# Float64 weights split by other VectorE and ScalarE operations without GpSimd, in a static issue order planned anew

## The chip, the cores and the metric

The kernel runs on one core of a Trainium2 chip. The metric is the device time of one execution in microseconds (us), as the median of several runs. TensorE is PE (PEld is its weight load), VectorE is DVE, ScalarE is ACT, GpSimd is POOL, and SyncE (SP) issues the transfers.

## The reference, cut to what matters

```
q, k = rotate(q), rotate(k)                    # rope; batch 2, 8 heads, 576 tokens, head size 64
attn = softmax(q @ k.T / 8) @ v                # (sum + 1e-9 below), float32
x = attn, heads side by side                   # 1152 x 512
h = x @ w_in                                   # 512 x 2048, float64 weights
g = h if h >= 1; 0 if h <= -1; else (h + 1)**2 / 4
x = (g @ w_out).astype(float32)                # 2048 x 512, float64 weights
p = domain_probs / (row sum + 1e-9)            # 1152 x 4
out = sum over 4 experts e of p[:, e] * (relu(x @ w1[e]) @ w2[e])   # inner width 1024, float32
```

## The kernel before

**Products.** Each operand of a product is cut into two float32r parts, high (h) and low (l), and each product is three matmuls: h·h, l·h, h·l. Activations stand as XH and XL, weights as pairs of tiles such as w00h and w00l.

**Units.** Attention works on 8 pairs of heads. For each: rope of k and q, their split, transposes, scores (tile `sc`), row maxima (`nm`), exponentials on ACT (`E`), transposed probabilities (`pt`, copied to `PT` and `PU`), the product with v (`av`), its scaling (`avx`) and its split to XH and XL. Probability sums take a round trip through DRAM (`rt`, `rdram`, `rbs`). The last product of attention is av71 (pair 7, second half). The feed-forward part has 12 chunks of the inner width: chunks 0 to 3 are the first layer pair (512 columns of `w_in` and 512 rows of `w_out` each), chunks 4 to 11 the four experts. Tokens stand in three column blocks of 384. A unit is one chunk and one block, once for the inward product (`pi`, four groups of twelve 128x384 matmuls) and once for the outward product (`po`). That makes 72 units. We write pi0_1 for chunk 0, block 1, and pi0_1_3 for its fourth group.

**After a pi group** of chunks 0 to 3 come two ACT operations (g?a), a DVE operation that reads PSUM (L438, g?b), an ACT cast (hid?h, L440) and a subtraction on POOL (hid?l, L441). A po group of chunks 1 to 3 is added to ACC on DVE (L478).

**Weights.** A float32 weight slice of 512 columns is split by one ACT copy and one DVE subtraction (L344). Float64 weights (32 slices, eight for each of chunks 0 to 3, four of `w_in` and four of `w_out`) arrive as pairs of 32-bit words in `wrawa` or `wrawb`, and `w_split` cuts each slice with the temporary tiles wt0 or wt1 (u and y each): L365 to L368 on DVE build a float32 y from the high words, ACT copies y to the h part (L381), L372 and L373 on DVE make the low words' value in u, POOL takes h from y (L377) and adds u to what remains (L385), which gives the l part. Chunk 0's slices are split during attention, the 24 others after it, in what we call the stage: from the end of av71 to the start of po2_0, the first outward unit of chunk 2.

**Order.** Every operation is registered with `op(engine, ns, priority, ...)`, and the class `Plan` runs a list scheduler over them before the program is emitted: its cost functions (`mm_ns`, `act_ns`, `dve_ns`, `pool_ns`), the constant LAT and the priorities in `CFG` fix in which order instructions stand on each engine and queue. Each engine then runs its list in that order. Tiles in rings (`Ring`) rotate. Phase 1 is what may only be issued once phase 0, attention, has been.

Of the kernel before, what the change touches and what calls it, by code (L numbers as in the profile page):

```python
# [10 lines left out]
F32 = mybir.dt.float32  # L11
# [7 lines left out]
P = 128  # L19
# [66 lines left out]
class Ring:  # L86
    """A rotating buffer: tiles take its slots in the order in which they are issued."""
# [24 lines left out]
class Op:  # L112
    __slots__ = ("eng", "ns", "fn", "prio", "bufs", "need", "outs", "ready", "lat", "seq", "phase", "start", "cols")


class Plan:
    """Static issue order: ops with their engine, length and data; a list scheduler over them."""

    LAT = 200.0
# [6 lines left out]
    def op(self, eng, ns, prio, fn, reads=(), writes=(), bufs=(), lat=0.0, phase=0, cols=None):  # L126
        o = Op()
        o.cols = ns * 2.37 if cols is None else cols
        o.eng, o.ns, o.fn, o.prio, o.bufs, o.lat, o.phase = eng, ns, fn, prio, bufs, lat, phase
# [12 lines left out]
        for d in deps:  # L142
            d.outs.append(o)
        o.need = len(deps)
        for b in bufs:
            b.left += 1
        self.ops.append(o)
        return o

    def order(self):  # L150
# [13 lines left out]
        heat, heat_to = CFG["fill"], CFG["fill_to"]  # L164

        def est(o):
            t = max(free[o.eng], o.ready)
# [12 lines left out]
            return t  # L180

        while len(out) < n:
# [72 lines left out]
def fused_kernel(ctx: ExitStack, tc, q, k, v, w_in, w_out, dprobs, w1, w2, tab, out):  # L255
# [67 lines left out]
    def w_split(c, kind, a, prio, phase, slot, tmp, after=()):  # L323
# [12 lines left out]
        def l():  # L336
            return part(1)

        if not is_wide(c):
            def t():  # L340
# [4 lines left out]
                l(), t(), h().bitcast(F32), op=ALU.subtract), [rk, hk], [lk], wb, phase=phase)  # L345
# [15 lines left out]
        def c1():  # L361
# [3 lines left out]
            nc.vector.tensor_scalar(uu, hi, 0x7FFFFFFF, None, op0=ALU.bitwise_and)  # L365
# [4 lines left out]
        def c2():  # L370
            u, y = uy()
            nc.vector.tensor_scalar(u.bitcast(U32), y.bitcast(U32), 0xFF800000, None, op0=ALU.bitwise_and)  # L372
            nc.vector.scalar_tensor_tensor(u, lohi()[0], 2.0 ** -52, u, op0=ALU.mult, op1=ALU.mult)  # L373

        def c3():
            y = uy()[1]
# [3 lines left out]
        op("DVE", 3 * dve_ns(512, True) + dve_ns(512) + 380, prio, c1, [rk], [uk, yk], phase=phase)  # L380
        op("ACT", act_ns(512, True), prio, lambda: nc.scalar.copy(h(), uy()[1]), [yk, *after], [hk], wb, phase=phase)  # L381
        op("DVE", dve_ns(512, True) + dve_ns(512) + 130, prio, c2, [rk, yk], [uk], phase=phase)
        op("POOL", pool_ns(512), prio, c3, [hk], [yk], phase=phase)
        e, ns = (nc.gpsimd, pool_ns(512)) if (CFG["ladd"][phase == 1] >> a & 1) else (nc.vector, dve_ns(512))
        op("POOL" if (CFG["ladd"][phase == 1] >> a & 1) else "DVE", ns, prio, lambda: e.tensor_tensor(l(), uy()[1], uy()[0], op=ALU.add),  # L385
           [yk, uk, hk], [lk], wb, phase=phase)
# [61 lines left out]
    def out_unit(c, b, d, ring, prio, phase):  # L448
# [82 lines left out]
        "PT0": Ring(kp, "PT0", 2, [P, 2, 4, 256], F32),  # L531
# [32 lines left out]
    def plan_pair(n):  # L564
# [23 lines left out]
        # loads  # L588
# [39 lines left out]
        def rope(x, eng, lo, hi, pr):  # L628
# [22 lines left out]
            op(engs[0], nss[0], pr, m1, rk + tk, sk, [raws[x], rot[x]])  # L651
            op(engs[1], nss[1], pr, m2, rk + tk, [(t2, lo)], [raws[x], t2])
            op(engs[2], nss[2], pr, m3, [(t2, lo)], sk, [rot[x], t2])

        def split_h(x, lo, hi, pr):
# [3 lines left out]
            if first:  # L659
# [14 lines left out]
            op("DVE", dve_ns(512, True) + dve_ns(64), pr, fn, rk, hk, [rot[x], hls[x]])  # L674

        def split_l(x, lo, hi, pr):
# [9 lines left out]
                op=ALU.subtract), rk + hk, lk, [rot[x], hls[x]])  # L686
# [102 lines left out]
        # scores, softmax, transposed probabilities  # L789
# [11 lines left out]
        def tile_step(s):  # L801
# [85 lines left out]
        def av(g):  # L887
# [13 lines left out]
            op("DVE", 270 + 75 * g, g0 + O["rd"], rd, [(sm, s) for s in range(lo, hi)], [r], [sm, r])  # L901
# [46 lines left out]
            op("DVE", dve_ns(256, True) + g * 102, te + O["xh"], xh, [ax], hk, [ax])  # L948
# [32 lines left out]
    # the tail columns of both batches form one column tile  # L981
# [25 lines left out]
    op("DVE", 790, 24, norm_probs, ["dpt"], ["probs"], phase=2)  # L1007
# [104 lines left out]
```

## Time and profile before

| | |
|---|---|
| median of 3 runs | 832.33 us (831.71 to 832.98) |
| the profiled execution, first to last instruction (span) | 831.0 us; no other time of that execution is given, and the median is 1.3 us above it |
| PE busy | 774.3 us (93%) |
| DVE, ACT, POOL busy | 476.5, 294.4, 257.5 us |
| bytes moved by transfers | 51 MB, 61 GB/s in the mean |

PE is busy in most of the span, but the share is a mean over stages: the span falls into attention (to 194.46 us), the stage that splits the rest of the float64 weights (to 340.78 us) and a rest of some 490 us.

### The profile page before, as it was taken

To read this page: it belongs to the slowest core of one execution; us is meant where nothing else is said; L and a number is where in the kernel's file an instruction comes from. 1 tells how busy PE (TensorE), PEld (TensorE's weight loads), DVE (VectorE), ACT (ScalarE), POOL (GpSimd) and SP (SyncE) were. 2 spreads that over 40 slices of the span, in tenths; PEclk is the share of its full clock that TensorE was granted. 3 is DMA by queue.
4 is the path that set the end of the run, shared out by engine and by line. 5 is a ranking of instruction groups with operands and counts; after the bars stand their busy time and mean duration, and the time that the engine had idled before them with its cause. 6 is when DMAs were issued, how large, how long until landed. Compare 5 with 4: busy or idle time off the path is not lost.

```text
span 831.0 us, 11155 instructions
## 1 busy us (share of the span) xinstructions
PE 774.3 (93%) x4310; PEld 691.4 (83%) x4310; DVE 476.5 (57%) x752; ACT 294.4 (35%) x663; POOL 257.5 (31%) x224
## 2 busy tenths in 40 slices
PE   5899999999876687799999999999999999999997
PEld 4677667789776687799999989998899899989996
DVE  6978798978999999734333333332433333332222
ACT  3677667664333332345531121220222121120110
POOL 4788773456656666522520000000000000000000
PEclk9999999999889999799999999999999999999999
DMA  5334333213232131211001111101111101000012
GB/s 162 96 97 125 97 75 108 82 67 108 95 102 101 52 102 50 102 52 51 26 26 50 51 52 51 44 8 50 51 51 52 38 14 51 1 1 1 1 38 77
DMA packets 38789, 51.08 MB, mean 61 GB/s; under 512 B 7624, under 2 KB 22288, under 8 KB 38736
## 3 DMA queue, kind: packets, MB, share of 16 engines
q1 hardware_dynamic: 38656, 50.04, 19.0%
q8 instruction: 34, 0.56, 0.3%
q0 software_dynamic: 80, 0.33, 0.2%
q14 instruction: 19, 0.16, 0.1%
HBM read 43.60 MB, written 2.40 MB: 55 GB/s over the span
## 4 chain that ended last, share of the span: by engine, by line
PE 73%; DVE 21%; issue 2%; ACT 1%; POOL 1%; DMA 1%; SPq 0%; DVEq 0%; POOLq 0%; ACTq 0%
PE pi L414 31%; PE po L466 30%; PE av L926 4%; PE sc L816 4%; PE pt L851 3%; DVE wt0u L366 2%; DVE wt1u L366 2%; DVE wt1u L365 2%; DVE wt0u L365 2%; DVE nm L833 1%; DVE wt0u L367 1%; DVE wt1u L367 1%; DVE XH L942 1%; DVE wt1y L368 1%; DVE wt0y L368 1%
## 5 line engine op out<-in xcount | busy, mean ns | idle before, releaser
L414 PE MATMUL pi<-XH,w 128*128 128x384 f32 x576 | 155.5, 345 | 18.8 <-DVE g2b L438 9.6
L414 PEld LDWEIGHTS pi<-XH,w 128*128 128x128 f32 x576 | 107.4, 191 | 21.3 <-DVE g2b L438 10.2
L414 PE MATMUL pi<-XH,w00h 128*128 128x384 f32 x288 | 98.0, 340 | 12.3 <-DVE g1b L438 9.4
L499 DVE SCALAR_TENSOR_TENSOR ACC<-po,ptile,ACC 128x512 f32<-128x512 f32 x63 | 47.3, 751 | 106.9 <-PE po L466 106.8
L414 PE MATMUL pi<-XL,w 128*128 128x384 f32 x288 | 99.0, 344 | 0.0
L414 PE MATMUL pi<-XH,w00l 128*128 128x384 f32 x288 | 97.1, 337 | 0.0
L414 PE MATMUL pi<-XL,w00h 128*128 128x384 f32 x288 | 97.0, 337 | 0.0
L414 PEld LDWEIGHTS pi<-XH,w00h 128*128 128x128 f32 x288 | 54.6, 190 | 14.6 <-DVE g1b L438 9.7
L833 DVE TENSOR_REDUCE nm<-sc 128x1 f32<-128x576 f32 x72 | 53.6, 748 | 14.7 <-PE sc L816 13.5
L466 PE MATMUL po<-w,hid0h 128*128 128x512 f32 x192 | 60.5, 396 | 0.0
L838 ACT ACTIVATE E<-sc,nm 128x576 f32<-128x576 f32 x72 | 53.6, 745 | 16.7 <-DVE nm L833 16.4
L466 PE MATMUL po<-w,hid2h 128*128 128x512 f32 x192 | 59.3, 390 | 0.0
L466 PE MATMUL po<-w,hid1h 128*128 128x512 f32 x192 | 59.3, 390 | 0.0
L414 PEld LDWEIGHTS pi<-XL,w 128*128 128x128 f32 x288 | 55.2, 192 | 0.5
L816 PE MATMUL sc<-K,Q 128*128 128x288 f32 x256 | 51.8, 329 | 3.9 <-ACT E L838 3.9
L414 PEld LDWEIGHTS pi<-XL,w00h 128*128 128x128 f32 x288 | 54.6, 190 | 0.4
L444 ACT ACTIVATE hid2h<-pi 128x384 fp32r<-128x384 f32 x32 | 15.7, 491 | 109.9 <-PE pi L414 109.9
L414 PEld LDWEIGHTS pi<-XH,w00l 128*128 128x128 f32 x288 | 54.6, 190 | 0.0
L444 ACT ACTIVATE hid0h<-pi 128x384 fp32r<-128x384 f32 x32 | 15.7, 491 | 105.3 <-PE pi L414 105.3
L816 PEld LDWEIGHTS sc<-K,Q 128*128 128x128 f32 x256 | 38.5, 200 | 16.7 <-ACT E L838 8.4
L445 DVE SCALAR_TENSOR_TENSOR hid0l<-pi,hid0h 128x384 fp32r<-128x384 f32 x32 | 17.8, 557 | 52.3 <-ACT hid0h L444 52.3
L851 PE MATMUL pt<-ident,E 128*128 128x128 f32 x288 | 42.1, 278 | 0.9 <-ACT PT L799 0.8
(185 smaller groups left out, 1623.3 us busy)
## 6 DMA issues: line engine op xcount, KB each, us to landing
wrawa<-in_moe_w_dram SPq DMA_DIRECT2D x8, 1024.0 KB
wrawb<-in_moe_w_dram SPq DMA_DIRECT2D x8, 1024.0 KB
wrawa<-in_moe_w_in_dram SPq DMA_DIRECT2D x5, 1024.0 KB
wrawa<-in_moe_w_out_dram SPq DMA_DIRECT2D x5, 1024.0 KB
K<-K SPq DMA_DIRECT2D x14, 304.0 KB
wrawb<-in_moe_w_in_dram SPq DMA_DIRECT2D x3, 1024.0 KB
wrawb<-in_moe_w_out_dram SPq DMA_DIRECT2D x3, 1024.0 KB
rawk<-in_k_dram SPq DMA_DIRECT2D x16, 128.0 KB
```

The source lines that it names most:

```text
L365: nc.vector.tensor_scalar(uu, hi, 0x7FFFFFFF, None, op0=ALU.bitwise_and)
L366: nc.vector.tensor_scalar(u, u, F64_MIN, F64_MAX, op0=ALU.max, op1=ALU.min)
L414: nc.tensor.matmul(ps()[:, 0:384], w[:, kt * P:(kt + 1) * P], x[:, kt, cols], start=(kt == 0 and m == 0), stop=(kt == 3 and m == 2))
L444: op("ACT", act_ns(384), prio, lambda: nc.scalar.activation(hh(), po(), AF.Relu), [pk], [hk], [ps], phase=phase)
L445: op("DVE", dve_ns(384), prio, lambda: nc.vector.scalar_tensor_tensor(hl(), po(), 0.0, hh().bitcast(F32), op0=ALU.max, op1=ALU.subtract), ...
L466: nc.tensor.matmul(ps()[:, 0:N], lh, rh, start=(kt == 0 and m == 0), stop=(kt == 3 and m == 2))
L499: op("DVE", 665, prio, lambda: nc.vector.scalar_tensor_tensor(acc(), ps()[:], pt[:, t, e:e + 1], acc(), op0=ALU.mult, op1=ALU.add), [pk, " ...
L816: nc.tensor.matmul(sc()[:, a, 0:288], lh, KK()[:, c0:c0 + 288], start=(x == 0), stop=(x == 1))
L833: op("DVE", 665, g0 + O["max"], lambda: nc.vector.tensor_reduce(nm(), pv(), axis=AX.XY, op=ALU.max, negate=True), [sc], [nm], [sc, nm])
L838: nc.scalar.activation(Et()[:, o0:o0 + 576].rearrange("p (a c) -> p a c", a=2), pv(), AF.Exp, bias=nm(), scale=1.0, accum_out=sm()[:, s:s ...
L851: nc.tensor.transpose(ps()[:, t * P:(t + 1) * P], Et()[:, c0 + t * P:c0 + (t + 1) * P], ident)
L926: nc.tensor.matmul(pa()[64 * j:64 * j + 64, 0:N], lh, rh, start=(t == 0), stop=(t == 4))
```

## The change

In `w_split`, the absolute value of the high words is taken on ACT (a lookup of Abs on the word read as float32) where DVE masked the sign bit. The low words no longer become a scaled float: an integer multiplication by 2^-29 with a minimum of 7 gives three bits, which are or-ed into y before ACT copies it; the l part is then y minus h, in one DVE subtraction. A slice takes six DVE and two ACT operations where it took six DVE, one ACT and two POOL ones.

The planner's model changes (matmul and transpose costs, LAT 200 to 140, and `port`: operations so marked on DVE, and POOL's, are planned so that they don't overlap), five rings (hl, K1, K2, Q1, PT0) take tiles in fixed order, and all priorities are replaced. The table `rp` moves four rope operations of pairs 5 to 7 (one m2 of k for pairs 5 and 6, the l part of k for pair 6, the m2 of q for pair 7) from POOL to DVE, `ev` takes two of four PT copies a pair from DVE to ACT, and `evu` brings one PU copy a pair from ACT to DVE.

```diff
 CFG = {
-    "eb": 3, "rp": [0, 7, 0, 0, 0, 0, 0, 0], "ord0": [0, 2, 1, 3, 4, 5, 6, 7, 8], "ev": 170, "evu": 0, ... "ladd": [15, 15], "ahead": 42.6,
+    "eb": 3, "rp": [64, 7, 0, 0, 0, 2, 66, 16], "ord0": [2, 0, 3, 1, 4, 5, 6, 7, 8], "ev": 9, "evu": 2, ... "ahead": 42.6,
...
-    return max(107, n / 2.4 + 3)
-T32, T32R = 109, 58
+    return max(86, n / 2.4 + 13.3)
+T32, T32R = 109, 87
...
-    LAT = 200.0
+    LAT = 140.0
...
         def est(o):
             t = max(free[o.eng], o.ready)
+            if o.port:
+                t = max(t, port[0])
...
             free[o.eng] = end
+            if o.port:
+                port[0] = end
...
         def c1():
-            nc.vector.tensor_scalar(uu, hi, 0x7FFFFFFF, None, op0=ALU.bitwise_and)
             nc.vector.tensor_scalar(u, u, F64_MIN, F64_MAX, op0=ALU.max, op1=ALU.min)
             nc.vector.tensor_scalar(uu, uu, 3, 0x3FFFFFFF, op0=ALU.logical_shift_left, op1=ALU.bitwise_and)
             nc.vector.scalar_tensor_tensor(y.bitcast(U32), hi, 0xC0000000, uu, op0=ALU.bitwise_and, op1=ALU.bitwise_or)
         def c2():
-            nc.vector.tensor_scalar(u.bitcast(U32), y.bitcast(U32), 0xFF800000, None, op0=ALU.bitwise_and)
-            nc.vector.scalar_tensor_tensor(u, lohi()[0], 2.0 ** -52, u, op0=ALU.mult, op1=ALU.mult)
-        def c3():
-            nc.gpsimd.tensor_tensor(y, y, h().bitcast(F32), op=ALU.subtract)
+            nc.vector.tensor_scalar(u.bitcast(U32), lohi()[0], 2.0 ** -29, 7.0, op0=ALU.mult, op1=ALU.min)
+            nc.vector.tensor_tensor(y.bitcast(U32), y.bitcast(U32), u.bitcast(U32), op=ALU.bitwise_or)
...
+        op("ACT", act_ns(512, True), prio, lambda: nc.scalar.activation(uy()[0], lohi()[1].bitcast(F32), AF.Abs), [rk], [uk], phase=phase)
...
-        op("POOL", pool_ns(512), prio, c3, [hk], [yk], phase=phase)
-        op("POOL" if (CFG["ladd"][phase == 1] >> a & 1) else "DVE", ns, prio, lambda: e.tensor_tensor(l(), uy()[1], uy()[0], op=ALU.add), ...)
+        op("DVE", dve_ns(512), prio, lambda: nc.vector.tensor_tensor(l(), uy()[1], h().bitcast(F32), op=ALU.subtract), ..., port=True)
```

On DVE, the instructions that follow the last attention operation (the XH casts of av71) are the first slices of chunk 1. Before:

```order
L365 TENSOR_SCALAR wt1u<-wrawa 128x512
L366 TENSOR_SCALAR wt1u<-wt1u 128x512
L367 TENSOR_SCALAR wt1u<-wt1u 128x512
L368 SCALAR_TENSOR_TENSOR wt1y<-wrawa,wt1u 128x512
L365 TENSOR_SCALAR wt0u<-wrawa 128x512
L366 TENSOR_SCALAR wt0u<-wt0u 128x512
L367 TENSOR_SCALAR wt0u<-wt0u 128x512
L368 SCALAR_TENSOR_TENSOR wt0y<-wrawa,wt0u 128x512
L372 TENSOR_SCALAR wt1u<-wt1y 128x512
L373 SCALAR_TENSOR_TENSOR wt1u<-wrawa,wt1u 128x512
```

At the same place now (lines of the changed kernel):

```order
L371 TENSOR_SCALAR wt1u<-wt1u 128x512
L372 TENSOR_SCALAR wt1u<-wt1u 128x512
L373 SCALAR_TENSOR_TENSOR wt1y<-wrawa,wt1u 128x512
L371 TENSOR_SCALAR wt0u<-wt0u 128x512
L372 TENSOR_SCALAR wt0u<-wt0u 128x512
L373 SCALAR_TENSOR_TENSOR wt0y<-wrawa,wt0u 128x512
L377 TENSOR_SCALAR wt1u<-wrawa 128x512
L378 TENSOR_TENSOR wt1y<-wt1y,wt1u 128x512
L377 TENSOR_SCALAR wt0u<-wrawa 128x512
L378 TENSOR_TENSOR wt0y<-wt0y,wt0u 128x512
L386 TENSOR_TENSOR w_2566<-wt1y,w_2566 128x512
```

The first operation of a slice is gone from DVE's list (it stands on ACT's), and the one that writes the l part (L386) has come to it from POOL's; all 24 slices of the stage stand behind av71 in both orders.

On PE, at the end of attention before (pi_1_3 is the last group of pi0_1, with the chunk's number left out):

```order
L414 MATMUL pi_1_3_2560<-XH,w00h 128x384
L414 MATMUL pi_1_3_2560<-XL,w00h 128x384
L414 MATMUL pi_1_3_2560<-XH,w00l 128x384
L926 MATMUL av_2583<-PT_2346,RV_99 64x320 x8
L926 MATMUL av_2583<-PU_2446,RV_99 64x320 x2
L414 MATMUL pi_2_0_2634<-XH,w00h 128x384
L414 MATMUL pi_2_0_2634<-XL,w00h 128x384
```

The same place now:

```order
L415 MATMUL pi_0_3_2466<-XH,w00h 128x384
L415 MATMUL pi_0_3_2466<-XL,w00h 128x384
L415 MATMUL pi_0_3_2466<-XH,w00l 128x384
L927 MATMUL av_2490<-PT_2226,RV_99 64x256 x8
L927 MATMUL av_2490<-PU_2300,RV_99 64x256 x2
L927 MATMUL av_2514<-PT_2319,RV_99 64x320 x8
L927 MATMUL av_2514<-PU_2450,RV_99 64x320 x2
L467 MATMUL po_0_0_2532<-hid0h,w_2259 128x384
L467 MATMUL po_0_0_2532<-hid0l,w_2259 128x384
```

One feed-forward unit (pi0_0) now stands in front of av71 where two (pi0_0, pi0_1) did, so pi0_1 has moved behind it: 13 units stand between av71 and po2_0 (po0_0, pi0_1, pi0_2, po0_1, po0_2, pi1_0, pi1_1, po1_0, pi1_2, po1_1, pi2_0, po1_2, pi2_1) where 12 did. From po2_0 on, the same 58 units follow.

At DVE's start before (t1k, t2k: rope of the first pair's k; its first part is 320 wide, its second 256):

```order
L642 TENSOR_TENSOR t1k_128<-rawk_115,tabs 128x320
L646 TENSOR_TENSOR t2k_131<-rawk_115,tabs 128x320
L650 TENSOR_TENSOR t1k_128<-t1k_128,t2k_131 128x320
L665 CAST hlk_first<-t1k_128 128x5x64
L684 TENSOR_TENSOR hlk_first<-t1k_128,hlk_first 128x5x64
L642 TENSOR_TENSOR t1k_128<-rawk_115,tabs 128x256
```

The same place now:

```order
L643 TENSOR_TENSOR t1k_133<-rawk_115,tabs 128x320
L643 TENSOR_TENSOR t1k_133<-rawk_115,tabs 128x256
L647 TENSOR_TENSOR t2k_143<-rawk_115,tabs 128x256
L685 TENSOR_TENSOR hlq_first<-t1q_125,hlq_first 128x3x64
L651 TENSOR_TENSOR t1k_133<-t1k_133,t2k_143 128x256
L647 TENSOR_TENSOR t2k_143<-rawk_115,tabs 128x320
```

The second part of k is now taken up before the first part is finished.

## Rows read from the trace of the kernel before

**Rows 1.** The page, busy time of each engine, share of the span, instructions.

```profile
PE 774.3 (93%) x4310; PEld 691.4 (83%) x4310; DVE 476.5 (57%) x752; ACT 294.4 (35%) x663; POOL 257.5 (31%) x224
```

**Rows 2.** Windows: length, busy PE, PEld, DVE, ACT, POOL (instructions), granted clock, DMA share, GB/s.

```profile
16.90:174.84 157.94, 149.90 (x1082) 112.30 (x1081) 136.31 (x249) 110.55 (x293) 105.78 (x87) 0.99 0.36 101
174.84:194.46 19.62, 19.28 (x122) 15.85 (x121) 13.19 (x28) 12.18 (x27) 10.93 (x12) 1.00 0.14 42
194.46:340.78 146.32, 112.30 (x579) 108.40 (x578) 141.59 (x177) 50.69 (x102) 95.88 (x72) 0.90 0.26 92
340.78:831.00 490.22, 485.31 (x2497) 448.72 (x2495) 175.57 (x279) 115.11 (x226) 35.95 (x34) 1.00 0.11 38
```

**Rows 3.** The tile av from 189 us: duration min/median/max, first and last start.

```profile
L926 PE MATMUL av<-PU,RV x4: 432/432/433, 193.8 to 194.1; 128*64 128x320 f32 x4
```

**Rows 4.** PE's waits, 195 to 345 us: in total, times, longest.

```profile
PE pi L414 <- DVE g1b L438: 11.4, 2, 9.4
PE pi L414 <- DVE g0b L438: 10.0, 3, 4.8
PE pi L414 <- DVE g2b L438: 9.6, 2, 7.3
```

**Rows 5.** The chain that ended last: start, length, work.

```profile
340.78 9.39 PE po L466 x48
350.18 8.33 PE pi L414 x48
...
826.13 0.75 DVE ACC L499
```

**Rows 6.** DVE's timeline early in the stage: start, duration, instruction.

```profile
199.75 0.42 DVE L365 TENSOR_SCALAR wt0u<-wrawa 128x512 uint32<-128x512 uint32 x1
200.21 0.43 DVE L366 TENSOR_SCALAR wt0u<-wt0u 128x512 f32<-128x512 f32 x1
200.67 0.43 DVE L367 TENSOR_SCALAR wt0u<-wt0u 128x512 uint32<-128x512 uint32 x1
201.13 0.69 DVE L368 SCALAR_TENSOR_TENSOR wt0y<-wrawa,wt0u 128x512 uint32<-128x512 uint32 x1
201.74 0.42 DVE L372 TENSOR_SCALAR wt1u<-wt1y 128x512 uint32<-128x512 uint32 x1
202.19 0.69 DVE L373 SCALAR_TENSOR_TENSOR wt1u<-wrawa,wt1u 128x512 f32<-128x512 uint32 x1
202.80 0.55 DVE L438 SCALAR_TENSOR_TENSOR g2b<-g2a,pi 128x384 f32<-128x384 f32 x1
```

**Rows 7.** The same timeline, one slice later.

```profile
212.87 1.51 DVE L365 TENSOR_SCALAR wt0u<-wrawb 128x512 uint32<-128x512 uint32 x1
214.42 1.40 DVE L366 TENSOR_SCALAR wt0u<-wt0u 128x512 f32<-128x512 f32 x1
...
218.11 1.52 DVE L365 TENSOR_SCALAR wt1u<-wrawa 128x512 uint32<-128x512 uint32 x1
```

**Rows 8.** Groups by line, 197 to 336 us: busy us, mean ns of one, idle before.

```profile
L478 DVE TENSOR_TENSOR ACC<-po,ACC 128x384 f32<-128x384 f32 x12 | 6.3, 548 | 0.0
L381 ACT CAST w<-wt0y 128x512 fp32r<-128x512 f32 x9 | 5.6, 622 | 34.6 <-DVE wt0y L368 34.6
```

**Rows 9.** Groups by line, the whole run.

```profile
L344 DVE TENSOR_TENSOR w00l<-wrawa,w00h 128x512 fp32r<-128x512 f32 x16 | 11.0, 690 | 2.6 <-ACT w00h L343 2.6
L441 POOL TENSOR_TENSOR hid0l<-g0b,hid0h 128x384 fp32r<-128x384 f32 x8 | 8.7, 1086 | 18.3 <-ACT hid0h L440 18.2
```

**Rows 10.** Timelines of SP and DVE: a load of wrawa, and its first reader.

```profile
191.89 0.38 SPq L320 DMA_DIRECT2D wrawa<-in_moe_w_in_dram  x1
...
197.18 1.00 DVE L365 TENSOR_SCALAR wt1u<-wrawa 128x512 uint32<-128x512 uint32 x1
```

**Rows 11.** DVE's timeline at the start, with the idle time before and its releaser.

```profile
5.93 0.49 DVE L642 TENSOR_TENSOR t1k<-rawk,tabs 128x320 f32<-128x320 f32 x1 [2.58 <-DMA rawk<-in_k_dram]
...
8.81 0.67 DVE L642 TENSOR_TENSOR t1k<-rawk,tabs 128x256 f32<-128x256 f32 x1
```

More of the change, by code (lines that the diff above doesn't have):

```diff
@@ L112 @@
 class Op:
-    __slots__ = ("eng", "ns", "fn", "prio", "bufs", "need", "outs", "ready", "lat", "seq", "phase", "start", "cols")
+    __slots__ = ("eng", "ns", "fn", "prio", "bufs", "need", "outs", "ready", "lat", "seq", "phase", "start", "cols", "port")
 class Plan:
-    LAT = 200.0
+    LAT = 140.0
     TICK, FULL = 3413.3, 3060.0
@@ L124, in __init__, with op @@
         self.wr, self.rd = {}, {}
-    def op(self, eng, ns, prio, fn, reads=(), writes=(), bufs=(), lat=0.0, phase=0, cols=None):
+    def op(self, eng, ns, prio, fn, reads=(), writes=(), bufs=(), lat=0.0, phase=0, cols=None, port=False):
         o = Op()
         o.cols = ns * 2.37 if cols is None else cols
+        o.port = port or (eng == "POOL" and lat == 0.0)
         o.eng, o.ns, o.fn, o.prio, o.bufs, o.lat, o.phase = eng, ns, fn, prio, bufs, lat, phase
@@ L164, in order @@
         heat, heat_to = CFG["fill"], CFG["fill_to"]
+        port = [0.0]
         def est(o):
             t = max(free[o.eng], o.ready)
+            if o.port:
+                t = max(t, port[0])
             if o.phase == 1 and left.get(0, 0):
@@ L371, in c2 @@
             u, y = uy()
[L372 to L377 removed]
+            nc.vector.tensor_scalar(u.bitcast(U32), lohi()[0], 2.0 ** -29, 7.0, op0=ALU.mult, op1=ALU.min)
+            nc.vector.tensor_tensor(y.bitcast(U32), y.bitcast(U32), u.bitcast(U32), op=ALU.bitwise_or)
         uk, yk = ("wtu", tmp), ("wty", tmp)
[L380 removed]
+        op("ACT", act_ns(512, True), prio, lambda: nc.scalar.activation(uy()[0], lohi()[1].bitcast(F32), AF.Abs),
+           [rk], [uk], phase=phase)
+        op("DVE", 2 * dve_ns(512, True) + dve_ns(512), prio, c1, [rk, uk], [uk, yk], phase=phase, port=True)
+        op("DVE", dve_ns(512, True) + dve_ns(512) + 130, prio, c2, [rk], [uk, yk], phase=phase, port=True)
         op("ACT", act_ns(512, True), prio, lambda: nc.scalar.copy(h(), uy()[1]), [yk, *after], [hk], wb, phase=phase)
[L382 to L386 removed]
+        op("DVE", dve_ns(512), prio, lambda: nc.vector.tensor_tensor(
+            l(), uy()[1], h().bitcast(F32), op=ALU.subtract), [yk, hk], [lk], wb, phase=phase, port=True)
     def load_probs():
@@ L673, in fn @@
                 nc.vector.tensor_copy(hl_view(x)[:, 8:9, 0, :], rot[x]()[:, 8:9])
-            op("DVE", dve_ns(512, True) + dve_ns(64), pr, fn, rk, hk, [rot[x], hls[x]])
+            op("DVE", dve_ns(512, True) + dve_ns(64), pr, fn, rk, hk, [rot[x], hls[x]], port=True)
         def split_l(x, lo, hi, pr):
@@ L685, in split_l @@
                 hl_view(x)[:, lo:hi, 1, :], rot[x]()[:, lo:hi], hl_view(x)[:, lo:hi, 0, :].bitcast(F32),
-                op=ALU.subtract), rk + hk, lk, [rot[x], hls[x]])
+                op=ALU.subtract), rk + hk, lk, [rot[x], hls[x]], port=True)
         def tail_copy(ps, KK, lo, hi, pr):
@@ L842, in tile_step @@
                 op("DVE", 102, g0 + O["exp"] + 0.1, lambda: nc.vector.tensor_copy(Et()[:, 576:640], Et()[:, 512:576]),
-                   [(Et, 0)], [(Et, 1)], [Et])
+                   [(Et, 0)], [(Et, 1)], [Et], port=True)
             ps = buf("pt", f"pt{n}_{s}")
@@ L900, in rd @@
                 nc.vector.reciprocal(r()[:, 0:nr], r()[:, 0:nr])
-            op("DVE", 270 + 75 * g, g0 + O["rd"], rd, [(sm, s) for s in range(lo, hi)], [r], [sm, r])
+            op("DVE", 270 + 75 * g, g0 + O["rd"], rd, [(sm, s) for s in range(lo, hi)], [r], [sm, r], port=True)
             ps = buf("pt", f"rb{n}{g}")
@@ L947, in xl @@
                                             XH[:, hp, d0:d0 + c1 - c0].bitcast(F32), op=ALU.subtract)
-            op("DVE", dve_ns(256, True) + g * 102, te + O["xh"], xh, [ax], hk, [ax])
+            op("DVE", dve_ns(256, True) + g * 102, te + O["xh"], xh, [ax], hk, [ax], port=True)
             op("POOL", pool_ns(256) + g * 283, te + O["xl"], xl, [ax] + hk, lk, [ax])
@@ L1006, in fused_kernel @@
     op("SP", 2000, 20, load_probs, writes=["dpt"], lat=2500.0, phase=2)
-    op("DVE", 790, 24, norm_probs, ["dpt"], ["probs"], phase=2)
+    op("DVE", 790, 24, norm_probs, ["dpt"], ["probs"], phase=2, port=True)
     psI = rings["pt"]
```

29 lines of the change are left out of this document (15 added, 14 removed), and 11 rows, old and new, of the table CFG.

## The prediction

> **What bounds the kernel now.** I read the page first: PE is busy in 93% of the span [rows 1], so at most 57 us are to be had without taking work from it. The windows then show where they lie [rows 2]. Attention's bulk has PE busy for 149.90 of 157.94 us, its end for 19.28 of 19.62, and the rest after 340.78 us for 485.31 of 490.22. The stage between, in which the remaining float64 weights are split, has it busy for only 112.30 of 146.32, at a granted clock of 0.90, while DVE is busy for 141.59. So the next view is PE's waits in that stage: three groups, each a pi group waiting for g on DVE, make 31.0 us, with single waits up to 9.4 [rows 4]. DVE's queue holds the splits ahead of these PSUM evacuations, so DVE bounds the stage, PE all else.
>
> The price of a unit comes from the chain. From 350.18 us, when the second unit after the stage starts, PE runs 57 units up to its end just before the last ACC at 826.13: 475.95/57 = 8.35 us each [rows 5]. The stage holds 12 units between av71 (which ends at 194.1 + 0.43 = 194.5 us [rows 3]) and 340.78, worth 12 x 8.35 = 100.2 us. It takes 146.3. **The 46 us of difference are what there is to win.**
>
> **DVE's price of a slice before.** Where nothing interferes, a slice's six operations follow each other from 199.75 to 202.80 us, that is 3.05 us: 0.46 from start to start for one input (0.42 to 0.43 long), 0.61 for two (0.69 long, the next begins 0.08 before its end) [rows 6]. Some 10 us later the same L365 takes 1.51 us, L366 1.40, and from one slice's L365 to the next 5.24 us pass [rows 7]. Something holds the operation, not its own work. Over the stage: 177 DVE instructions [rows 2] are 23 slices of six, 33 evacuations and six others. At the free prices, 23 x 3.05 + 33 x 0.47 (548 ns less the overlap of 0.08 [rows 8]) + 1.5 = 87.2 us; DVE is busy for 141.6. The 54.4 us above that, over the 95.88 us in which POOL is busy, are **0.57 us held per us of POOL**.
>
> That is a mean, so a page may be set beside it. The Trainium skill ("GPSIMD Engine Reference", section 1, the specifications) says that GpSimd shares its SBUF interfaces with VectorE, and that DVE instructions in a 2-port mode or with two SBUF inputs contend. The rule speaks against expecting all of the 46 us: the six operations left are still of these kinds, and POOL keeps the hid subtractions. If each of those held DVE for its full length, the stage's wait below would be 19.4 us in place of 6.3, and the whole 804. The evacuations at 548 ns, with one input from PSUM [rows 8], agree with the rule.
>
> **The change: the stage after it.** The new order has 13 units on PE between av71 and po2_0: 13 x 8.35 = 108.6 us. Of DVE's six operations per slice, three are L366 to L368 of before (0.46 + 0.46 + 0.61). L377 reads strided words as L365 does but computes, a form that the trace doesn't have: bounds 0.45 (as L372, one input) and 0.72 (by the 0.69 us of L373, which computes on the same words); I take 0.45, since it has a single input as all operations at 0.42 have. L378 and L386 have two inputs as L344, 0.69 us long [rows 9], so 0.61 each. Sum 3.20 us; it isn't fewer DVE operations that bring the time, but POOL's absence. 24 slices are 76.8 us, and 28 + 12 evacuations (28 g, 12 ACC in the new order) 40 x 0.47 = 18.8. POOL keeps 28 hid subtractions of 1.09 us [rows 9], 30.5 us, which at 0.57 hold DVE for 17.4. Together 113.0 us.
>
> Its first slice waits for a load. Before, the load issued at 191.89 has its first reader at 197.18, so it lands within 5.3 us [rows 10]. The new order issues it after the last low-words operation of chunk 0, some 2 us before av71's end, and Abs on ACT (0.62 us, as its copies [rows 8]) comes between: DVE starts about 4 us after av71. So DVE needs 117.0 us where PE needs 108.6; PE works on one more group while DVE empties the last, and runs so far ahead, 8.35/4 = 2.1 us. **PE's waits in the stage: 117.0 - 108.6 - 2.1 = 6.3 us.** Bounds: 2 if nothing is held and only the start waits, 19.4 if each hid subtraction holds in full (30.5 for 17.4), and 6.5 more if L377 costs 0.72 (24 x 0.27). What is late next is PE.
>
> ACT has in the stage 24 Abs more, 14.9 us, beside 50.69 busy of 146 us: hidden, as long as no Abs stands in front of a g in its list while its load is under way (rival C).
>
> **The change: attention.** One unit stands before av71 in place of two: 194.5 - 8.35 = 186.1 us. POOL loses the 16 split operations of chunk 0 and four rope operations; DVE loses the L365 of eight slices, two PT copies a pair and gets eight L386, a PU copy a pair and the four rope operations. ACT gets eight Abs and one copy a pair net, some 9 us at 0.62 and below, on 110.55 busy of 157.94 [rows 2], so it keeps room. PE idles there for 8.04 us [rows 2], the most that lighter POOL and DVE can return; I take 3, over a third, since POOL's splits are the part that held DVE. Against it stands the start: DVE's third instruction is now the second part of k, which before it could begin only at 8.81 us, where the first part began at 5.93 [rows 11]; what completes the first part now stands behind it. Up to 2.9 us and some reordering, 0 to 4; I take 2.5. So av71 ends at 186.1 - 0.5 = **185.6 us** (bounds 178, all idle time gone, to 190).
>
> **The rest.** From po2_0's start 831.0 - 340.78 = 490.2 us pass to the end. Its first unit took 9.39 us against 8.35 [rows 5], right behind the last wait; with shorter waits I take that 1.0 off: 489.1. The weights there are float32, split as before; the 58 units are the same.
>
> **Sum.** 185.6 + 108.6 + 6.3 + 489.1 = 789.6 us of span. The median before is 1.3 above the span, so **791 us**, 0.95 of before. By term against before: attention -8.35 (a unit moved) - 0.5, stage 146.3 to 114.9, rest -1.0. All unknown bounds at once would be 779 to 815; they are independent, so taken as squares (-7.6 and -4.1 down; +4.4, +13.1, +6.5 up) the main case covers 782 to 806.
>
> **Rivals.**
>
> A: *DVE stays the bound.* Full holds and the dear L377: 76.8 + 6.5 + 18.8 + 30.5 + 4 = 136.6, less 108.6 and 2.1, is a wait of 25.9 for 6.3, so 811 us (up to 817 with evacuations at 0.55). For it: L365 at 1.51 us, longer than a hid subtraction [rows 7]. Against: the mean was 0.57 per us of POOL, and POOL was busy in two thirds of the stage without holding any operation of [rows 6].
>
> B: *Attention also gains fully, DVE is no bound.* All 8.0 us of idle gone, start free, waits at nothing: 791 - 7.6 - 6.3 = 777 (774 to 780). For it: POOL is busy for 105.78 of 157.94 us [rows 2] and loses work. Against: in attention PE's chain passes through maxima, exponentials and copies, which stay.
>
> C: *Slower.* Abs stands in ACT's list ahead of exponentials and PT copies, and waits for the load of its words; ACT goes no further, PE gets no probabilities. A load takes up to 5.3 us [rows 10]; chunk 0 has four. If nothing hides them, 4 x 5.3 = 21 us, 812 in all. Slower than 832 it gets from 10.3 us per load on. The Trainium skill ("TensorE: Matmul & The Clock Gate", its table of figures) gives ScalarE a strictly ordered queue, so what stands behind an Abs can't overtake; no row before shows an Abs. Against: each load is issued when the slices before it have been read, which need DVE time, and the order puts several ACT operations between.
>
> D: *It makes no difference.* POOL's holding would have to be DVE's own slowness: 24 slices at 5.24 us [rows 7] without any POOL splits. Only a contender outside POOL (a DMA) could do that; 26% share in the stage, but 36% in attention [rows 2] and rows 6 within the same stage speak against it.
>
> **How the numbers follow.** Main 0.76, A 0.12, B 0.07, C 0.03, D 0.02. The time is the main case's 791. The range for 8 in 10 takes in its 782 to 806, half of A above and most of B below: 774 to 812. A change of this kernel under 0.2% (1.7 us) can't be told from none. Main, A and B are all faster: 0.95; D the same: 0.02; C slower beyond its point: 0.03.
>
> **What would show it.** Right: DVE's split operations at 0.42 to 0.69 us in most of the stage, the held ones only under hid subtractions; po2_0 starting at about 300 us (185.6 + 114.9); PE's waits for g below 10 us; the granted clock near 1; 58 units of 8.35 after. Wrong: L377 at 0.6 us or above, hid subtractions that hold several DVE operations in a row (A); ACT idle on a wrawa load with exponentials behind it, and av71 after 190 us (C); av71 before 180 (B); L371 still at 1.4 us with POOL idle (D).

## The result and the profile after

The changed kernel takes 795.47 us (median of 4 runs, 794.01 to 795.93) against 832.02 (4 runs): a ratio of 0.956, 95% interval 0.9543 to 0.9577. The forecast was 791 with a range of 774 to 812. The profiled execution took 794.01 us, of which its span is 792.0; it lies 1.5 us below the median.

The page of the changed kernel, busy time of each engine (against [rows 1]), and its windows, for the stage and for the rest, with the columns of [rows 2]:

```profile
PE 766.8 (97%) x4319; PEld 685.5 (87%) x4319; DVE 419.7 (53%) x748; ACT 317.2 (40%) x703; POOL 160.5 (20%) x156
```

```profile
184.84:302.75 117.91, 112.10 (x625) 110.51 (x626) 104.01 (x185) 70.91 (x140) 31.38 (x28) 0.99 0.34 114
302.75:792.00 489.25, 484.38 (x2496) 447.86 (x2495) 172.35 (x276) 114.89 (x225) 31.38 (x31) 1.00 0.11 38
```

The windows lie on the two places of the prediction: av71 ends at 184.84 us, and po2_0 starts at 302.75. PE's share went from 93 to 97%. In the stage POOL is busy for 31.4 us instead of 95.9, DVE for 104.0 instead of 141.6 with one unit more to serve, and the granted clock is back at 0.99, near the upper of its two levels (2.4 GHz). The rest is 489.25 us, against 490.22.

The chain that ended last, three of its pieces (start, length, work; against [rows 5]), gives the place of the units: 58 of them run from 302.75 to 787.15, 8.352 us each.

```profile
184.84 8.68 PE po L467 x48
...
302.75 8.48 PE po L467 x48
...
770.79 16.36 PE po L467 x72
```

PE's waits in the stage, against [rows 4], where the same groups were 31.0 us:

```profile
PE pi L415 <- DVE g0b L439: 4.5, 2, 2.3
PE pi L415 <- DVE g1b L439: 1.0, 1, 1.0
PE pi L415 <- DVE g2b L439: 0.2, 1, 0.2
```

PE is idle for 5.8 us of this stage (117.91 - 112.10), where it was idle for 34.0. That isn't all: PE is busy for 112.10 us with 13 units, and was for 112.30 with 12, which at 8.35 us each are 108.6 and 100.2. So units ran longer too, above all at a lower granted clock. The group that follows the wait ending at 282 us shows it: 3.91 us, where a group takes 8.35/4 = 2.1, at a clock of 0.56.

```profile
282.17:286.08 3.91, 3.91 (x13) 3.91 (x14) 3.58 (x6) 2.17 (x5) 1.70 (x2) 0.56 0.01 4
```

DVE's timeline where nothing interferes (the operations of a slice in wt1 alternate with those of its neighbours in wt0, six in a turn):

```profile
221.51 0.69 DVE L386 TENSOR_TENSOR w<-wt1y,w 128x512 fp32r<-128x512 f32 x1
222.11 0.42 DVE L371 TENSOR_SCALAR wt1u<-wt1u 128x512 f32<-128x512 f32 x1
222.56 0.43 DVE L372 TENSOR_SCALAR wt1u<-wt1u 128x512 uint32<-128x512 uint32 x1
223.02 0.69 DVE L373 SCALAR_TENSOR_TENSOR wt1y<-wrawa,wt1u 128x512 uint32<-128x512 uint32 x1
223.63 0.68 DVE L386 TENSOR_TENSOR w<-wt0y,w 128x512 fp32r<-128x512 f32 x1
224.23 0.42 DVE L377 TENSOR_SCALAR wt1u<-wrawa 128x512 uint32<-128x512 uint32 x1
224.69 0.69 DVE L378 TENSOR_TENSOR wt1y<-wt1y,wt1u 128x512 uint32<-128x512 uint32 x1
225.30 0.42 DVE L371 TENSOR_SCALAR wt0u<-wt0u 128x512 f32<-128x512 f32 x1
```

From one L371 to the next pass 225.30 - 222.11 = 3.19 us, where the prediction had 3.20. L377, the form that the trace of before didn't have, takes 0.42 us. What is left of the holds shows where POOL has a hid subtraction. POOL's timeline, and DVE's at the same time:

```profile
236.10 1.02 POOL L442 TENSOR_TENSOR hid0l<-g0b,hid0h 128x384 fp32r<-128x384 f32 x1 [20.24 <-ACT hid0h L441]
237.08 1.21 POOL L442 TENSOR_TENSOR hid0l<-g1b,hid0h 128x384 fp32r<-128x384 f32 x1
```

```profile
235.81 0.42 DVE L371 TENSOR_SCALAR wt1u<-wt1u 128x512 f32<-128x512 f32 x1
236.26 1.15 DVE L372 TENSOR_SCALAR wt1u<-wt1u 128x512 uint32<-128x512 uint32 x1
237.44 1.39 DVE L373 SCALAR_TENSOR_TENSOR wt1y<-wrawa,wt1u 128x512 uint32<-128x512 uint32 x1
238.76 0.68 DVE L386 TENSOR_TENSOR w00l<-wt0y,w00h 128x512 fp32r<-128x512 f32 x1
```

Here each of the two POOL operations holds one DVE operation, which ends 0.3 to 0.5 us after POOL's: L372 takes 1.15 us for 0.43 and L373 1.39 for 0.69, 0.7 us each. Evacuations, which read PSUM, are not held: L479 takes 549 ns in the mean over the stage, as L478 did [rows 8]. Over the whole stage the groups of DVE by line (busy us, mean ns of one) show how much is held, against 0.43 us free for L372 and 0.69 for the others:

```profile
L378 DVE TENSOR_TENSOR wt0y<-wt0y,wt0u 128x512 uint32<-128x512 uint32 x12 | 9.8, 816 | 0.4
L378 DVE TENSOR_TENSOR wt1y<-wt1y,wt1u 128x512 uint32<-128x512 uint32 x12 | 9.0, 750 | 0.4
L386 DVE TENSOR_TENSOR w<-wt0y,w 128x512 fp32r<-128x512 f32 x10 | 7.8, 784 | 1.4 <-ACT w L385 1.4
L372 DVE TENSOR_SCALAR wt1u<-wt1u 128x512 uint32<-128x512 uint32 x12 | 7.4, 615 | 0.4
...
L373 DVE SCALAR_TENSOR_TENSOR wt0y<-wrawa,wt0u 128x512 uint32<-128x512 uint32 x6 | 6.2, 1038 | 0.2
```

Together, with L371 (511 ns in wt0) and the smaller groups, the splits were held for 10.5 us. Of the 28 hid subtractions 26 fall into the stage: 30.3 us of POOL, 1.17 us each, where 28 of 1.09 were forecast. Set beside DVE's timeline, 13 of the 26 hold a split operation by 0.7 to 0.8 us, three hold one by less, and ten hold none. No split operation of this stage is held while POOL is idle, nor is any in the stage of before.

### The profile page after: what moved, and what is told of

Same layout as the page of the kernel before. It is cut to its first block, busy times and chain, and to the rows that moved or that the text cites. A ratio compares the mean times of both kernels' runs of the same rounds, so it can differ in the third digit from the quotient of the medians.

```text
span 792.0 us, 11132 instructions
## 1 busy us (share of the span) xinstructions
PE 766.8 (97%) x4319; PEld 685.5 (87%) x4319; DVE 419.7 (53%) x748; ACT 317.2 (40%) x703; POOL 160.5 (20%) x156
## 4 chain that ended last, share of the span: by engine, by line
PE 86%; DVE 9%; ACT 2%; issue 1%; DMA 1%; SPq 0%; POOL 0%; DVEq 0%
PE po L467 36%; PE pi L415 35%; PE av L927 5%; PE sc L817 4%; PE pt L852 3%; DVE nm L834 1%; PE sc L827 1%; DVE w L386 1%; ACT E L839 1%; DVE wt0u L372 1%; DMA rawq<-in_q_dram 1%; PE pu L878 1%; PE pstq L702 1%; PE pstk L702 1%; DVE wt1u L372 0%
## 5 line engine op out<-in xcount | busy, mean ns | idle before, releaser
L415 PE MATMUL pi<-XH,w 128*128 128x384 f32 x576 | 152.3, 339 | 3.6 <-DVE g0b L439 2.3
L415 PEld LDWEIGHTS pi<-XH,w 128*128 128x128 f32 x576 | 105.1, 188 | 5.3 <-DVE g0b L439 2.6
L445 ACT ACTIVATE hid2h<-pi 128x384 fp32r<-128x384 f32 x32 | 15.7, 491 | 109.9 <-PE pi L415 109.9
L445 ACT ACTIVATE hid0h<-pi 128x384 fp32r<-128x384 f32 x32 | 15.7, 491 | 105.3 <-PE pi L415 105.3
L817 PEld LDWEIGHTS sc<-K,Q 128*128 128x128 f32 x256 | 37.6, 197 | 16.9 <-ACT E L839 5.9
L467 PEld LDWEIGHTS po<-w,hid0h 128*128 128x128 f32 x192 | 36.1, 188 | 8.1
```

Of the source, the lines that this page charges most:

```text
L415: nc.tensor.matmul(ps()[:, 0:384], w[:, kt * P:(kt + 1) * P], x[:, kt, cols], start=(kt == 0 and m == 0), stop=(kt == 3 and m == 2))
L445: op("ACT", act_ns(384), prio, lambda: nc.scalar.activation(hh(), po(), AF.Relu), [pk], [hk], [ps], phase=phase)
L467: nc.tensor.matmul(ps()[:, 0:N], lh, rh, start=(kt == 0 and m == 0), stop=(kt == 3 and m == 2))
L817: nc.tensor.matmul(sc()[:, a, 0:288], lh, KK()[:, c0:c0 + 288], start=(x == 0), stop=(x == 1))
```

## The experiments

To compare the kernels, one number is worked out alike for each: **the loss behind av71**, the time from av71's end to PE's end, less the units that stand in it at 8.35 us. For before that is 826.11 - 194.53 - 70 x 8.352 = 46.9 us, for the changed kernel 787.15 - 184.84 - 71 x 8.352 = 9.3 (split_alone has 69 units there, stage_split_only 70, all others 71). The last column is the part of this loss in which PE is idle. What remains is units that run longer: 1.5 to 2.1 us in the three kernels whose granted clock stays at 1.00 through the stage (l_on_pool, defer_l_on_pool, hid_on_dve), 3.5 to 12.9 us in all others, where it falls behind waits. Times are medians, but these columns stand on one profiled execution each. All ratios are against the kernel before.

```
kernel               median us   ratio (95% interval)       av71 ends   loss behind it  idle PE
before               832.02      1                          194.53      46.9           34.0
changed              795.47      0.956  (0.9543 to 0.9577)  184.84       9.3            5.8
split_alone          821.84      0.9884 (0.9869 to 0.9898)  218.63      19.5           14.5
plan_alone           838.65      1.0076 (1.0054 to 1.0097)  200.53      38.6           31.5
stage_split_only     800.32      0.9624 (0.9608 to 0.9640)  194.73      14.3           10.0
abs_on_dve           801.22      0.9631 (0.9615 to 0.9647)  186.43      16.2           11.3
l_on_pool            792.44      0.9531 (0.9517 to 0.9545)  186.23       7.3            5.2
pool_twice           804.67      0.9678 (0.9654 to 0.9702)  188.23      18.6           12.1
cost_270             795.11      0.9567 (0.9548 to 0.9587)  184.23       9.2            5.5
l_on_pool_cost_270   795.64      0.9572 (0.9558 to 0.9586)  187.73       8.7            3.9
defer_chunk3         796.48      0.9582 (0.9568 to 0.9596)  185.03      11.0            6.5
defer_l_on_pool      793.15      0.9549 (0.9532 to 0.9565)  185.43       7.8            5.8
defer_cost_270       798.47      0.9613 (0.9596 to 0.9630)  184.83      12.1            8.6
hid_on_dve           788.16      0.9483 (0.9469 to 0.9497)  185.23       3.3            1.8
```

### One half of the change at a time

**split_alone**: the old table and planner with the new `w_split`.

> The kernel before with the new split of a slice alone; its priorities and planner costs stay. The planner now puts three units before av71 and 11 between av71 and po2_0. Theory (POOL's split operations held DVE, and that is the gain): DVE's demand in the stage falls to 76.8 us for 24 slices at 3.20, some 16 for evacuations, 9 to 17 of holds and 4 for the first load, 105 to 113 us; with av71 near 200 us (one unit more, 3 us of idle returned) and 489 behind it, 790 to 808 us. Rival (the new order brings the gain, the split little): 822 to 835 us.

821.84 us, between the two: above the theory's 790 to 808, and just under the rival's 822. The loss behind av71 fell to 19.5 us, as the theory has it, but av71 ended at 218.63, where a unit more than before would have put it at 202.9: attention got 15.7 us longer. It isn't the Abs waiting for its load; that wait is in none of ACT's or PE's groups. PE's waits before av71 are spread over many places:

```profile
PE sc L811 <- ACT E L833: 5.8, 5, 1.9
PE rb L898 <- DVE r L895: 4.5, 3, 1.8
PE pstq L696 <- DVE PT L792: 2.6, 2, 1.8
PE sc L821 <- ACT E L833: 2.4, 1, 2.4
```

**plan_alone**: the new table and planner with the old `w_split`.

> The changed kernel with the old split of a slice: POOL takes y - h and + u again; priorities, planner and moved rope operations stay new. Theory (the holds come back): the stage takes about 146 us or some more as it did, av71 ends at 186 to 190 us, in all 815 to 845 us, with DVE's L366-like operations at 1.4 us again. Rival (the new order brings the gain): 795 to 805 us.

838.65 us, 0.8% slower than before. The loss is back (38.6 us), and L372, which is L366 of before, takes 1.05 us in the mean for 0.43:

```profile
L372 DVE TENSOR_SCALAR wt1u<-wt1u 128x512 f32<-128x512 f32 x11 | 11.6, 1053 | 0.4
```

A single wait of 21.4 us, po on POOL's hid0l, is now its largest piece. And here too attention ends 15.7 us later than in the changed kernel. With either half alone, then, attention is 15.7 us longer; the next kernel leaves attention as it was.

**stage_split_only**: the kernel before, the new split for `phase == 1` alone.

```diff
+        if phase == 1:
...
+            return
...
```

Behind the condition stand the new split's operations, as in the changed kernel; the old split follows the `return`.

> The kernel before with the new split for the 24 slices of the stage alone; attention's eight slices keep the old one, and all that stands before av71 stands as it did (two units before av71, 12 between it and po2_0). Theory (the split is the gain, and what the split alone lost in attention came from priorities made for other slices): av71 at 194.5 us as before, the stage 100.2 us of units and 5 to 12 of waits, in all 791 to 798 us, as fast as the whole change. Rival (the new priorities and costs are needed in the stage too): the stage keeps half of its 46 us of loss or more, 808 us or above.

800.32 us, 2 us above what the theory gave and 8 below the rival. The loss goes from 46.9 to 14.3 us with the old priorities in the same 12 units, and av71 stands where it stood. So the split in the stage brings 31 of the 36 us, which leaves 5 to the new order and attention's slices.

### What is it that holds DVE

**abs_on_dve**: in the stage, the mask on DVE again.

```diff
+            if phase == 1:
+                nc.vector.tensor_scalar(uu, hi, 0x7FFFFFFF, None, op0=ALU.bitwise_and)
...
+        if phase != 1:
+            op("ACT", act_ns(512, True), prio, lambda: nc.scalar.activation(uy()[0], lohi()[1].bitcast(F32), AF.Abs),
...
```

> The changed kernel with the absolute value of the 24 slices of the stage as a DVE mask again, not on ACT. Theory (DVE still sets what the stage takes over PE's 108.6 us): DVE gets 24 x 0.46 = 11 us more and the time rises by 7 to 11 us, to 802 to 807. Rival (what is left of the waits comes from the order or from ACT, DVE has room): within 2 us of the changed kernel, 793 to 798, or faster, since ACT is rid of 16 us.

801.22 us, 5.8 more, a little under the theory's 7 to 11; the loss grew by 6.9 of the 11 us that DVE got, and PE's idle time by 5.5. DVE is still what PE waits for, but it isn't full: it is busy for 113.5 of the 124.8 us of this stage.

**pool_twice**: each hid subtraction of `phase == 1` issued twice. That is 24 of the 28: pi0_1 was planned with chunk 0 and isn't in that phase, which the expectation overlooked.

```diff
-            op("POOL", ..., lambda: nc.gpsimd.tensor_tensor(hl(), GAB[gab][1], hh().bitcast(F32), op=ALU.subtract), ...)
+            def sub():
+                for _ in range(2 if phase == 1 else 1):
+                    nc.gpsimd.tensor_tensor(hl(), GAB[gab][1], hh().bitcast(F32), op=ALU.subtract)
+            op("POOL", ..., sub, ...)
```

> The changed kernel with each of POOL's 28 hid subtractions of the stage issued twice, so 30.5 us more of POOL's work at the same places, on DVE the same order. Theory (POOL holds DVE by a part of its time, 0.34 us per us in the changed kernel's stage): 10 us more of held DVE operations, of which the stage passes on most, 800 to 807 us. Rival one (what holds DVE is its own wait on data, not POOL): 794 to 798 us. Rival two (full hold): 815 us and above.

804.67 us. The stage alone (loss 18.6 for 9.3; the median holds a later av71 too, see the last section):

```profile
188.23:315.45 127.22, 115.08 (x625) 113.45 (x626) 115.34 (x184) 70.73 (x139) 57.27 (x49) 0.96 0.31 106
```

DVE has the same instructions in the same order as in the changed kernel and is busy for 115.3 us instead of 104.0: 11.3 us held for 25.9 us more of POOL, 0.44 per us. That shows the cause: POOL's work lengthens DVE's.

**l_on_pool**: the last subtraction of the stage's slices back on POOL.

```diff
-        op("DVE", dve_ns(512), prio, lambda: nc.vector.tensor_tensor(l(), uy()[1], h().bitcast(F32), op=ALU.subtract), ...)
+        le, ln, e = ("POOL", pool_ns(512), nc.gpsimd) if phase == 1 else ("DVE", dve_ns(512), nc.vector)
+        op(le, ln, prio, lambda: e.tensor_tensor(l(), uy()[1], h().bitcast(F32), op=ALU.subtract), ...)
```

> The changed kernel with the last subtraction of the 24 slices of the stage (y - h, the l part) on POOL. DVE loses 24 x 0.61 = 14.6 us, POOL gets 24 operations of about 1.4 us, 34 us. Theory (POOL's work holds DVE at 0.34 to 0.57 us per us): 11 to 19 us held come back, the sum is -4 to +5 us, 791 to 801. Rival one (fewer DVE operations are what counts): the 9 us of waits vanish, 785 to 788. Rival two (each POOL operation holds DVE in full): +15 us and more, 810 to 815.

792.44 us, as the theory had it, with a loss of 7.3. PE's idle time is 5.2 us there, for 5.8: most of the 2.0 us by which the loss is smaller comes with the granted clock, which stays at 1.00 in this execution. A subtraction costs 0.61 us on DVE; on POOL it holds a DVE operation by 1.0 (L373 takes 1.67 to 1.70 us for 0.69), but only where it meets one. Two places on DVE's timeline:

```profile
221.22 1.70 DVE L373 SCALAR_TENSOR_TENSOR wt1y<-wrawb,wt1u 128x512 uint32<-128x512 uint32 x1
...
225.01 1.67 DVE L373 SCALAR_TENSOR_TENSOR wt0y<-wrawb,wt0u 128x512 uint32<-128x512 uint32 x1
```

**hid_on_dve**: the hid subtractions of `phase == 1` (24 of 28 again) on DVE, so that POOL does nearly nothing.

```diff
-            op("POOL", pool_ns(384), prio, lambda: nc.gpsimd.tensor_tensor(
+            se, sn, e = ("DVE", dve_ns(384), nc.vector) if phase == 1 else ("POOL", pool_ns(384), nc.gpsimd)
+            op(se, sn, prio, lambda: e.tensor_tensor(
                 hl(), GAB[gab][1], hh().bitcast(F32), op=ALU.subtract), ...)
```

> The changed kernel with the 28 hid subtractions of the stage on DVE, so that POOL does nothing there and holds nothing. Theory (holds of 0.34 us per us of POOL): DVE gets 28 x 0.47 = 13 us and loses 10 of holds, in all +1 to +5 us, 796 to 801 us, and every split operation at 0.42 to 0.69 us. Rival one (operations are held by something besides POOL): 806 us and above, with operations at 1.2 to 1.4 us left. Rival two (full holds of 30 us): 785 us or below.

788.16 us, 0.9483 (0.9469 to 0.9497): **faster than both kernels**, where the theory had it 1 to 5 us slower, and above the 785 of rival two. Its stage, and three of DVE's groups there:

```profile
185.23:297.13 111.90, 110.13 (x625) 108.89 (x626) 104.60 (x207) 72.12 (x140) 6.26 (x6) 1.00 0.36 122
```

```profile
L378 DVE TENSOR_TENSOR wt0y<-wt0y,wt0u 128x512 uint32<-128x512 uint32 x12 | 8.3, 692 | 0.4
L378 DVE TENSOR_TENSOR wt1y<-wt1y,wt1u 128x512 uint32<-128x512 uint32 x12 | 8.3, 692 | 0.4
...
L443 DVE TENSOR_TENSOR hid0l<-g0b,hid0h 128x384 fp32r<-128x384 f32 x4 | 2.2, 553 | 0.1
```

The holds are gone, but for those of the four subtractions that stay on POOL (L378 at 692 ns in both groups; in the changed kernel 816 and 750). DVE is busy for 104.6 us, as it was (104.0): what it took over, it got back. But the stage is 6.0 us shorter, so its sum isn't what sets the loss. Of the 6.0 us, 4.0 are idle time of PE (1.8 us for 5.8), and 2.0 are units that ran longer in the changed kernel (PE busy for 110.13 us, for 112.10).

### Is it the order in the stage

In the changed kernel DVE is busy for 94% of 188.26 to 286 us, and idles afterwards:

```profile
188.26:286.00 97.74, 91.93 (x511) 90.34 (x510) 92.26 (x160) 60.63 (x120) 25.06 (x22) 0.98 0.34 113
286.00:302.75 16.75, 16.75 (x98) 16.75 (x97) 10.62 (x21) 9.24 (x19) 5.31 (x5) 1.00 0.21 65
```

**cost_270** and **l_on_pool_cost_270**: a truer price for a slice in the planner, on the changed kernel and on l_on_pool.

```diff
-        op("DVE", 2 * dve_ns(512, True) + dve_ns(512), prio, c1, ...)
+        op("DVE", 2 * dve_ns(512, True) + dve_ns(512) + 270 * (phase == 1), prio, c1, ...)
```

> The changed kernel with 270 ns more as the planner's price of a stage slice's first DVE part (1.53 us from start to start in the trace, 1.26 in the plan); nothing else. Theory (the 9 us left in the stage come from slices that stand ahead of g evacuations, as the planner takes DVE to be quicker than it is): evacuations move ahead, PE's waits fall by 3 to 7 us, 788 to 793 us. Rival (DVE's work in sum sets the stage, in whatever order): within 1.5 us of the changed kernel, 794 to 797 us.

> The last subtraction of the stage's slices on POOL, and 270 ns more as the planner's price of a slice's first DVE part. Theory (less DVE work and an order by its true price add up): 1 to 4 us less than with the subtraction on POOL alone, 788 to 791 us. Rival (the operations that POOL holds come at places that no fixed price tells, so the order gains nothing): 791 to 794 us.

795.11 and 795.64 us: no gain (losses 9.2 and 8.7, from 9.3 and 7.3). The first is as its rival had it, the second above both of its ranges. In cost_270 one wait of 5.1 us stands in place of four. On l_on_pool the price did cut PE's idle time, from 5.2 to 3.9 us, but the granted clock fell in the stage of this execution (0.97 in the mean to 305 us, for 1.00), and the loss rose.

**defer_chunk3**, **defer_l_on_pool**, **defer_cost_270**: chunk 3's slices planned after pi2_0.

```diff
+        late = [("pi", 2, 0, 3)] if c == 3 else []
...
-           [rk], [uk], phase=phase)
+           [rk, *late], [uk], phase=phase)
...
-                if jc < 2 or last.get(("out" if jk else "in", jc - 2), -1) <= i:
+                if jc < 2 or (last.get(("out" if jk else "in", jc - 2), -1) <= i and (jc != 3 or i >= at20)):
```

> The changed kernel with chunk 3's eight slices planned no earlier than after pi2_0; nothing else. Theory (DVE is full from 188 to 286 us, and part of what it does there, chunk 3's slices from 259 us on, isn't needed before pi3_0, after the stage, where DVE has room): of the 9 us that the stage takes over its units those that come after 247 us go, 789 to 793 us. Rival one (a slice put off is paid for where it lands): within 1.5 us of the changed kernel, 794 to 797. Rival two (the waits all come from chunk 2's slices ahead of pi1_0's evacuations): within 2 us too, with the waits near 235 and 246 us unchanged.

> Chunk 3's slices put off as above, and the last subtraction of the stage's slices on POOL. Theory (both take work from DVE where it is full, and add): 786 to 791 us, under each of the two alone. Rival (POOL's holds take back what it does for DVE; nothing over deferral alone): 789 to 793 us.

> Chunk 3's slices put off, and the planner's price of a slice's first DVE part 270 ns up. Theory (with chunk 3 gone DVE has room from 250 us on, so what is left are chunk 2's slices ahead of pi1_0's evacuations, and a truer price moves those): 1 to 3 us under deferral alone. Rival (pricing moved nothing before and moves nothing now): within 1.5 us of deferral alone.

796.48, 793.15 and 798.47 us: nothing over the same kernels without it, and some 2 us lost where both edits meet; none of the three theories held. The wait moved on: in defer_chunk3 the one near 235 us stays (2.47), those at 246 and 282 are gone, and new ones of 1.16 and 2.85 us stand at 298 and 318, where chunk 3's slices now are. Rival one was right: a slice put off is paid for where it lands.

## Why the prediction was right

**What bounds the kernel.** Right. plan_alone shows that with POOL's split operations the loss of the stage stays (38.6 of 46.9 us), stage_split_only that without them most of it goes (14.3). Rival D, that the change makes no difference, is out with it. The 46 us to be won were not all waits, though: from before to the changed kernel the loss fell by 37.6 us, of which 28.2 were idle time of PE and 9.4 came from units that had run longer.

**The price of a slice.** 3.20 forecast, 3.19 measured; L377 at the lower of its two bounds.

**Holds.** 17.4 us forecast. The split operations were held for 10.5 us: 0.35 per us of POOL's 30.3 us of hid subtractions, not 0.57. The mean of before came mostly from operations of 1.4 to 1.6 us, and DVE's timeline beside POOL's shows that each of the 47 split operations that POOL began in the stage of before met a split operation of DVE; of the hid subtractions in the changed kernel's stage ten in 26 met none that they held. The rule of the Trainium skill that was weighed against it ("GPSIMD Engine Reference", section 1) names VectorE instructions in a 2-port mode or with two SBUF inputs. The trace agrees as far as it shows them: those held have SBUF operands alone, two inputs (L373) or one (L372, whose mode no row shows), and none that reads PSUM is held. The section gives no part; full holds, 804 us, were too much.

**The stage.** This is the step that failed in its form and nearly held in its number: 114.9 us forecast, 117.9 measured, with 9.3 us beyond the units in place of 6.3. Of the 9.3 us, 5.8 are idle time of PE, close to the 6.3; the other 3.5 are units that ran longer than 8.35 us, for which the sum had no term. That the idle time came so close is luck. PE's wait was taken as DVE's work in sum against PE's. With the measured holds and the measured start (DVE began 3.4 us after av71, forecast 4) that sum is 76.6 + 18.8 + 10.5 + 3.4 = 109.3, which would leave PE no wait. The too large hold stood in for something that the sum doesn't have: DVE idles for 13.9 us of the stage (2.3 of them for the first slice's Abs), while PE waits earlier for evacuations behind slices. hid_on_dve shows the same from the other side, with equal DVE work, an idle PE for 1.8 us and a loss of 3.3. Neither a truer price for the slices nor putting chunk 3's off took the loss away. What stays open is which part of hid_on_dve does it: it takes out the holds, which no plan foresees, it has a shorter subtraction on the way from g to po (0.55 us for 1.2 in the mean, though none of PE's waits in the changed kernel's stage is for it), and it is planned in another order. These weren't told apart.

**Attention.** av71 was forecast at 185.6 and ended at 184.84. The start was right. PE's timeline, the first score of the kernel before and of the changed one:

```profile
15.58 2.25 PE L816 MATMUL sc<-K,Q 128*128 128x288 f32 x8
```

```profile
17.97 0.37 PE L817 MATMUL sc<-K,Q 128*128 128x288 f32 x1
```

It begins 2.4 us later, for 2.5 forecast. So the 3 us given back were 3.7 (194.53 - 8.35 + 2.4 - 184.84). But the runs below show that one execution tells av71 no better than to some us. What split_alone and plan_alone show, 15.7 us of attention lost with either half alone, the prediction didn't have; that priorities planned for one kind of slices fit the other badly is argued, not shown.

**The rest and the sum.** 489.25 for 489.1. In all the span came out 2.4 us above the forecast (-0.8 attention, +3.0 stage, +0.2 rest), the time around the span 0.7 (2.0 for 1.3), and the profiled execution 1.5 below the median: together the 4.5 us between 791 and 795.47.

**Rivals.** A, that DVE stays the bound at 811, would have needed full holds and an L377 of 0.69. Its upper end of 817 doesn't follow from its terms: 40 evacuations at 0.08 more are 3.2 us, so 814. And the argument against it from [rows 6] says little, since POOL stood idle through most of that stretch, to 202.30 us:

```profile
202.30 1.74 POOL L377 TENSOR_TENSOR wt1y<-wt1y,w 128x512 f32<-128x512 f32 x1 [3.94 <-ACT g2a L436]
```

B needed av71 before 180 us. C, an Abs that stops ACT while its load is under way, didn't show: PE's waits on E are 2.2 us in the changed kernel in all, 3.9 before.

## What to carry to other kernels

Before work is shared out between VectorE and GpSimd, read VectorE's durations while GpSimd runs: here a GpSimd subtraction of 1.2 us in the mean made the SBUF operation of VectorE that it met, in 13 cases of 26, 0.7 to 0.8 us longer, more than the 0.47 us that VectorE needs to do the subtraction itself. New operations and a new plan are to be measured apart, too: here either half alone cost 16 us in attention, for a reason that stays open. And a sum of work tells what an engine can do, not that its queue has the right thing in front: check a stage against the idle time of the engine that is said to bound it.

## What the runs showed that was not expected

Ten of the kernels, the changed one among them, have the same instructions in the same order on every engine up to av71, and yet av71 ended between 184.2 and 188.2 us in their profiles. It goes with PE's granted clock from 16 to 50 us. The same window of cost_270, of the changed kernel and of pool_twice, with the clock as the third number from the end:

```profile
16.00:50.00 34.00, 30.55 (x204) 24.32 (x206) 26.84 (x50) 25.25 (x68) 22.33 (x17) 1.00 0.43 116
```

```profile
16.00:50.00 34.00, 30.29 (x206) 23.73 (x205) 27.79 (x50) 25.29 (x68) 22.57 (x17) 0.90 0.42 117
```

```profile
16.00:50.00 34.00, 29.22 (x186) 24.26 (x187) 24.88 (x44) 22.61 (x61) 20.70 (x15) 0.80 0.35 99
```

At 1.00 av71 ended at 184.23 us, at 0.80 at 188.23; the five kernels at 0.90 lie at 184.8 to 186.4, the three at 0.85 at 185.4 to 187.7. The clock is at its lower level, 1.2 GHz, for more or less of the first scores. So a difference of 2 us between two of these kernels is told by the stage in their profiles, as above, rather than by their medians.
